# A fused attention, mixture-of-experts and feed-forward kernel: weight pieces kept in DRAM, work moved from GpSimd to VectorE, and plain products in half of the output layers

## The chip, the cores and the metric

The kernel runs on one core of a Trainium2 chip. A core has TensorE (PE, matmuls, with PEld its weight loads), VectorE (DVE), ScalarE (ACT), GpSimd (POOL) and SyncE (SP, which issues transfers); each works through its own queue in order. The metric is the device time of one execution in microseconds, and less is better.

## The reference

Three layers follow each other. Linear attention gives x of 2304 tokens by 512; four experts, weighted by probabilities, give the next x; a feed-forward layer with a sigmoid gate gives the output.

```python
q_s = softmax(q over the head dim);  k_s = softmax(k over the sequence)
x   = q_s @ (k_s.T @ v)                          # 4 batches, 8 heads of 64, 576 tokens
p   = domain_probs / domain_probs.sum(-1)
x   = sum over e of p[:, e] * (relu(x @ w1[e]) @ w2[e])    # 4 experts, 512 -> 1024 -> 512
h   = x @ w_in                                   # 512 -> 2048
out = (h * sigmoid(1.702 * h)) @ w_out           # 2048 -> 512
```

w_in and w_out arrive as 64-bit floats.

## The kernel before, in words

Tokens are taken in three passes of 768 (`TP`), each as two halves of 384 (`N`). Weights are taken in units of 512 hidden columns: eight units a pass in the expert layers (`moe`, two for an expert), four in the last layer (`ffn`), so 24 + 12 = 36 units. A unit is a first layer (`mm1`, two halves of 256 hidden columns) and an output layer (`mm2`, two halves `dt` of 256 output columns).

Each half multiplies a 2x2 arrangement of weight blocks (a11 to a22) by a 2x2 arrangement of activations (b11 to b22). It does so with seven block products where eight would be the plain way: sums of weights s1 to s4 (`MADE`) and of activations t1 to t4 (`TSUM`) take part, `ORDER` (L111) lists the products with the PSUM bank that each adds to ("x", "z" or "y"), and a bank is read several times while products add up in it. For accuracy every factor is split into a rounded part and its residue: ScalarE casts (`hi`), and a subtraction gives the rest (`lo`). A product is six matmuls of 128x128 by 128x384 (`product`, L117): two blocks of the inner dimension times high-high, high-low and low-high.

`weights_of` (L136) makes the pieces of a half. At the first pass GpSimd makes the sums s1 to s4, ScalarE casts all seven pieces, DVE makes the residues of the sums and of a22, GpSimd those of a11 and a12, and the four sums' pieces are stored to DRAM. At the later passes the raw block is loaded again, the four sums are reloaded ready-made, and a11, a12 and a22 are cast and their residues made by GpSimd again. `x_forms` (L209) and `h_forms` (L300) do the like for activations: seven casts, seven residues on DVE, and t1 and t2 on DVE and t3 and t4 on GpSimd for the hidden ones.

The outputs of `mm2` add up in `acc` over the units of an expert (first copies on ScalarE, adds on DVE); `weigh` multiplies by the probabilities on GpSimd and `total` adds to `tot` on DVE.

In the background of the expert passes run the attention for the later tokens and the decoding of w_in and w_out to 32 bits (32 tiles, seven DVE operations and a GpSimd add each). Generators give them out a turn at a time; `pump` asks for the next turn. All attention turns, the transposes of the output and the "y" products share three "y" banks.

The order is written by hand: `at(place, fn)` puts work on a plan in steps, a step being one product of each layer, and the plan is sorted by place and emitted as it is. `mm2` runs 4 steps (`LAG`) behind the unit's end, so the output layer of one unit and the first layer of the next alternate on PE. A piece's steps are given relative to the step that uses it:

```python
at(slot - 11, load)
...
            if x in MADE:
                if again:
                    at(s - 6, reload, x)
                    continue
                at(s - 7, make, x, SUM_ENG[x])
            at(s - 5, hi, x)
            at(s - 3.9, lo, x, (LO_AGAIN if again else LO_ENG)[x])
            if x in MADE:
                at(s - 2.2, store, x)
```

Of the kernel before, what the change touches and what calls it, by code (L numbers as in the profile page):

```python
# [22 lines left out]
def tile_linear_attention_moe_gelu(  # L23
# [49 lines left out]
    BANKS = {"x": 3, "z": 2, "y": 3}  # L73
# [43 lines left out]
    def product(st, i, weights, forms, nm):  # L117
        w, f, b, first = ORDER[i]
        if first:
            st[b] = bank(b, [P, N], f"{b}{nm}")  # L120
        (wh, wl), (xh, xl) = weights.pop(w), forms[f]
        n = 0
        for kk in range(2):
            for l, r in ((wh, xh), (wh, xl), (wl, xh)):
                T.matmul(  # L125
                    st[b], l[:, kk, :], r[:, kk, :], start=(first and n == 0), stop=(n == 5),
                    skip_group_check=True,
                )
                n += 1
# [6 lines left out]
    def weights_of(key, nm, src, slot):  # L136


        got, y, made = {}, {}, {}
        again = key in kept  # L140
        names = [x[0] for x in ORDER]

        def load():
            y["raw"] = rawp.tile([P, KT, 256], F32, tag="raw", name=f"raw{nm}")
            S_.dma_start(out=y["raw"], in_=src.rearrange("(c p) f -> p c f", p=P))

        def block(x):
# [24 lines left out]
        def store(x):  # L172
            d = dram.tile([P, 512], F32, name=f"k_{x}_{nm}")
            kept[key][x] = d
            S_.dma_start(out=d, in_=y[x])

        def reload(x):
            flat = new(x)
            S_.dma_start(out=flat, in_=kept[key][x])

        at(slot - 11, load)
        for i, x in enumerate(names):
            s = slot + i
            if x in MADE:
                if again:
                    at(s - 6, reload, x)
                    continue
                at(s - 7, make, x, SUM_ENG[x])
            at(s - 5, hi, x)
            at(s - 3.9, lo, x, (LO_AGAIN if again else LO_ENG)[x])  # L190
            if x in MADE:
                at(s - 2.2, store, x)
        if not again:
            kept[key] = {}
        return got

    SUM_ENG = {"s1": G, "s2": G, "s3": G, "s4": G}
    LO_ENG = {"a11": G, "s1": V, "s2": V, "a12": G, "s3": V, "s4": V, "a22": V}
    LO_AGAIN = {"a11": G, "a12": G, "a22": G}
# [9 lines left out]
    def x_forms(pas_key, nm, slot, source, S=G):  # L209
# [26 lines left out]
        at(slot - 2.6, make, "t3", G, "b12")  # L236
# [16 lines left out]
    def mm1(kx, layer, pas, half, slot, weights):  # L253
# [29 lines left out]
        for i in range(7):  # L283
            at(slot + i, lambda i: product(st, i, weights, X[layer, pas], nm), i)
# [15 lines left out]
    def h_forms(kx, s1):  # L300

        forms = Hf[kx] = {}
        place = {}

        def src(f):
            return U[kx, place.get(f, f)]

        def hi(f):
            forms[f] = form_tiles(pools["hp", "p"], f, f"_{kx}")
            A.copy(forms[f][0], src(f))  # L310

        def lo(f, eng):
            tt(eng, forms[f][1], src(f), forms[f][0].bitcast(F32), ALU.subtract)
# [6 lines left out]
        at(s1 + 6.20, hi, "b11")  # L320
        at(s1 + 6.70, lo, "b11", V)
        at(s1 + 7.30, make, "t1", V, "b11")
        at(s1 + 7.35, make, "t3", G, "b12")
        at(s1 + 7.90, hi, "t1")
        at(s1 + 8.30, lo, "t1", V)
        at(s1 + 9.30, make, "t2", V, "b11")
        at(s1 + 9.80, hi, "t2")
        at(s1 + 10.30, lo, "t2", V)
        a, b = ("t3", "b21") if kx + 1 < len(seq) else ("b21", "t3")
        at(s1 + 10.80, hi, a)  # L330
        at(s1 + 11.30, lo, a, V)
        at(s1 + 11.80, hi, b)
        at(s1 + 12.30, lo, b, V)
        at(s1 + 12.80, hi, "b22")
        at(s1 + 12.85, make, "t4", G, "b21")
        at(s1 + 13.30, lo, "b22", V)
        at(s1 + 14.00, hi, "t4")
        at(s1 + 14.40, lo, "t4", V)
# [10 lines left out]
    def mm2(kx, layer, pas, u, dt, slot, weights):  # L349
# [18 lines left out]
        for i in range(7):  # L368
            at(slot + i + 0.5, lambda i: product(st, i, weights, Hf[kx], nm), i)
        for i, (r, t, b) in enumerate(  # L370
            ((0, 0, "x"), (1, 1, "z"), (0, 1, "x"), (0, 0, "y"), (1, 1, "x"), (0, 1, "z"), (1, 0, "x"))
        ):
            at(slot + i + 1.05, add, r, t, b)
# [11 lines left out]
        def total(r):  # L385
            kk = 2 * dt + r
            if e:
                o = acc[dt, r].rearrange("p t n -> p (t n)")
                tt(V, tot[pas][:, kk, :], tot[pas][:, kk, :], o, ALU.add)
            if e == E - 1:  # L390
                S_.dma_start(out=x_d["ffn", pas][:, kk, :], in_=tot[pas][:, kk, :])

        def turn(x, eng):

            y = bank("y", [SP, 2, 2, P], f"o{nm}_{x}")
# [7 lines left out]
            S_.dma_start(  # L403
# [6 lines left out]
        if layer == "moe" and last:  # L410
            for r, s in ((0, 6.3), (1, 7.4)):
                at(slot + s, weigh, r)
                at(slot + s + 3 + 0.9 * r, total, r)
        if layer == "ffn" and last:
            for n, x in enumerate((2, 3, 0, 1)):
                at(slot + (6.6, 7.2, 7.6, 7.9)[n], turn, x, V if n % 2 and kx == len(seq) - 1 else A)
# [3 lines left out]
    seq = [(layer, p, u) for layer, n in (("moe", E * FE // FU), ("ffn", FF // FU)) for p in range(NPASS) for u in range(n)]  # L420
    begins = {}
    for kx, (layer, pas, u) in enumerate(seq):
# [3 lines left out]
        if layer == "moe":  # L426
            e, f0 = divmod(u * FU, FE)
            wa, wb = w1[e], w2[e]
        else:
            f0, wa, wb = u * FU, wi32, wo32  # L430
        for half in range(2):
            sl = s0 + 7 * half
            got = weights_of(
                (layer, u, 1, half), f"a{kx}_{half}", wa[:, f0 + half * 256 : f0 + (half + 1) * 256],
                sl if kx else START + 17 + 7 * half,
            )
            mm1(kx, layer, pas, half, sl, got)
        h_forms(kx, s0 + 7)
        for dt in range(2):
# [3 lines left out]
            got = weights_of((layer, u, 2, dt), f"b{kx}_{dt}", wb[f0 : f0 + FU, dt * 256 : (dt + 1) * 256], sl)  # L443
            mm2(kx, layer, pas, u, dt, sl, got)
        if layer == "moe" and u % 2 == 0:
            at(s0 + 18, load_p, u // 2, pas)


    def attend(b, j, c0, nc_, keys):
# [14 lines left out]
        def bk(n, s):  # L464
            return bank(ATTN_BANK[early].get(n, "y"), s, f"{n}_{nm}")

# [170 lines left out]
        def group(g):  # L637
# [16 lines left out]
            def xf(eng):  # L654
# [39 lines left out]
    ATTN_BANK = {True: {"kT0": "x", "kT1": "x", "kb0": "z", "kb1": "z"}, False: {}}  # L694
# [28 lines left out]
    def probabilities():  # L723
# [13 lines left out]
        def turn(x):  # L737
            w = 4 * SP
            y = bank("y", [E, w], f"pt{x}")
# [4 lines left out]
            S_.dma_start(out=pt_d[:, x * w : (x + 1) * w], in_=o)  # L744
# [52 lines left out]
    def attention(todo):  # L797
# [12 lines left out]
        while live:  # L810
# [4 lines left out]
            if todo and len(live) < 2 and (not live or len(live[0]) == 4):  # L815
                nxt = load(todo.pop(0))
                live.append([(nxt[0][0], "")] * 2 + nxt)
# [48 lines left out]
    def decode_all(part):  # L866
# [4 lines left out]
        for n, x in enumerate(todo):  # L871
            if n + 1 < len(todo):
                next(todo[n + 1])
            for stage, _ in enumerate(x):
                yield
                if stage == 1 and late:
# [75 lines left out]
```

## Time and profile before

| | |
|---|---|
| median of 3 runs | 1468.76 us (1466.09 to 1469.67) |
| the profiled execution | 1470.22 us, its span 1468.4 us |
| mean granted TensorE clock | 0.931 |
| instructions | 21252 |
| DMA | 292.46 MB, mean 199 GB/s |

The span is the time from the first to the last instruction. Busy time is the time in which an engine executes; waiting, branching and issuing transfers don't count. In a window of the trace the busy time of each engine can be set beside the window's length. An operation's duration can overlap the next one's start on the same engine, so the sum of durations is more than the busy time.

### The profile page before, as it was taken

The numbers are of one execution on the slowest core, as the hardware profiler recorded it, in microseconds if no ns is written. First come the engines' busy times: TensorE is split into PE (matmuls) and PEld (weight loads), VectorE is DVE, ScalarE is ACT, GpSimd is POOL, SyncE is SP. The second block draws the span as 40 slices with busy tenths as digits, with TensorE's granted clock in tenths as the row PEclk, the third lists the DMA queues.
The fourth block names the chain that finished last, engine by engine and source line by source line (L and its number), as shares of the span: only waits on it lengthen the run. The fifth ranks groups of instructions, "written<-read, shape, count | busy, mean of one in ns | idle before, by whom it ended". The sixth has DMA issues, their size and how long they took to land.

```text
span 1468.4 us, 21252 instructions
## 1 busy us (share of the span) xinstructions
PE 1243.8 (85%) x6688; PEld 1191.0 (81%) x6688; DVE 1320.2 (90%) x1779; ACT 762.5 (52%) x1715; POOL 963.3 (66%) x805
## 2 busy tenths in 40 slices
PE   7778878797798997778877778998888779989998
PEld 6677877697798987778867777997788679989997
DVE  6779999999998889999999999878999997898787
ACT  5566564474655653344534344555565546555653
POOL 5267877778856765658665665769876754564552
PEclk8799988899899998899988989999989999999999
DMA  8145555455568786668667766775455547776773
GB/s 222 57 160 179 195 173 168 141 190 182 188 205 261 222 283 206 191 229 269 192 205 266 244 212 212 224 240 170 157 181 172 201 143 252 216 234 202 224 214 86
DMA packets 208383, 292.46 MB, mean 199 GB/s; under 512 B 34296, under 2 KB 122640, under 8 KB 207632
## 3 DMA queue, kind: packets, MB, share of 16 engines
q1 hardware_dynamic: 208272, 291.11, 62.1%
q8 instruction: 53, 0.87, 0.2%
q14 instruction: 58, 0.48, 0.1%
HBM read 219.71 MB, written 71.34 MB: 198 GB/s over the span
## 4 chain that ended last, share of the span: by engine, by line
DVE 49%; PE 32%; issue 9%; ACT 4%; POOL 3%; DMA 2%; SPq 0%; DVEq 0%; POOLq 0%; ACTq 0%
PE x L125 18%; PE z L125 8%; DVE acc L108 6%; DVE b L108 6%; PE y L125 4%; DVE t1l L108 3%; DVE s_a L108 3%; DVE s_b L108 2%; DVE t3l L108 2%; DVE tot L108 2%; DVE b11l L108 2%; DVE t2l L108 2%; DVE b22l L108 1%; DVE e L108 1%; DVE p L108 1%
## 5 line engine op out<-in xcount | busy, mean ns | idle before, releaser
L108 POOL TENSOR_TENSOR b<-b,b 128x768 f32<-128x768 f32 x72 | 139.2, 1933 | 201.3 <-DVE b21l L108 113.8
L108 POOL TENSOR_TENSOR a_b<-rawb,a_b 128x256 fp32r<-128x256 f32 x192 | 209.6, 1092 | 42.3 <-ACT a_b L166 42.2
L108 POOL TENSOR_TENSOR a_a<-rawa,a_a 128x256 fp32r<-128x256 f32 x192 | 204.0, 1062 | 17.8 <-ACT a_a L166 16.4
L125 PE MATMUL x<-t4h,a_b 128*128 128x384 f32 x288 | 97.5, 380 | 70.5 <-DVE acc L108 70.2
L125 PE MATMUL x<-t3h,s_b 128*128 128x384 f32 x288 | 92.6, 363 | 39.5 <-DVE acc L108 32.2
L125 PEld LDWEIGHTS x<-t4h,a_b 128*128 128x128 f32 x288 | 58.9, 208 | 81.6 <-DVE acc L108 81.5
L108 DVE TENSOR_TENSOR acc<-x,acc 128x384 f32<-128x384 f32 x198 | 108.1, 546 | 10.6 <-PE x L125 10.2
L125 PE MATMUL x<-t4h_moe,a_a 128*128 128x384 f32 x192 | 63.5, 372 | 49.0 <-DVE e L108 49.0
L125 PE MATMUL x<-t2h,s_b 128*128 128x384 f32 x288 | 94.5, 370 | 5.7 <-DVE acc L108 4.4
L125 PEld LDWEIGHTS x<-t3h,s_b 128*128 128x128 f32 x288 | 55.8, 197 | 48.9 <-DVE acc L108 35.6
L310 ACT CAST t2h<-b 128x768 fp32r<-128x768 f32 x36 | 30.1, 837 | 119.8 <-DVE b L108 119.8
L125 PE MATMUL x<-b11h,a_b 128*128 128x384 f32 x288 | 91.3, 358 | 0.0
L108 POOL TENSOR_TENSOR acc<-acc,pb 128x768 f32<-128x768 f32 x36 | 73.6, 2049 | 26.6 <-DVE acc L108 26.6
L166 ACT CAST a_a<-rawa 128x256 fp32r<-128x256 f32 x216 | 86.9, 402 | 0.0
L166 ACT CAST a_b<-rawb 128x256 fp32r<-128x256 f32 x216 | 86.9, 403 | 0.0
L125 PE MATMUL z<-b22h,s_b 128*128 128x384 f32 x288 | 86.5, 341 | 0.0
L125 PE MATMUL z<-t1h,s_b 128*128 128x384 f32 x288 | 84.9, 335 | 0.1
L125 PE MATMUL y<-b21h,a_b 128*128 128x384 f32 x288 | 84.8, 335 | 0.0
L125 PEld LDWEIGHTS x<-t4h_moe,a_a 128*128 128x128 f32 x192 | 37.8, 200 | 55.7 <-DVE e L108 55.5
L276 ACT ACTIVATE b<-p 128x384 f32<-128x384 f32 x48 | 25.2, 526 | 106.3 <-DVE p L108 106.2
L108 DVE TENSOR_TENSOR b<-b,b 128x768 f32<-128x768 f32 x72 | 79.1, 1098 | 0.1
L108 DVE TENSOR_TENSOR acc<-z,acc 128x384 f32<-128x384 f32 x114 | 62.3, 547 | 18.0 <-PE z L125 17.9
(266 smaller groups left out, 4700.7 us busy)
## 6 DMA issues: line engine op xcount, KB each, us to landing
s_a<-k_s_a SPq DMA_DIRECT2D x192, 256.0 KB, 3.9
s_b<-k_s_b SPq DMA_DIRECT2D x192, 256.0 KB, 3.8
rawa<-in_moe_w SPq DMA_DIRECT2D x48, 512.0 KB, 5.3
k_s_a<-s_a SPq DMA_DIRECT2D x96, 256.0 KB, 2.3
rawb<-in_moe_w SPq DMA_DIRECT2D x48, 512.0 KB, 5.7
k_s_b<-s_b SPq DMA_DIRECT2D x96, 256.0 KB, 2.5
rawa<-wi SPq DMA_DIRECT2D x24, 512.0 KB, 4.9
rawb<-wo SPq DMA_DIRECT2D x24, 512.0 KB, 4.3
```

The source lines that it names most:

```text
L108: eng.tensor_tensor(out=o, in0=a, in1=b, op=op)
L125: T.matmul(st[b], l[:, kk, :], r[:, kk, :], start=(first and n == 0), stop=(n == 5), skip_group_check=True,)
L166: A.copy(got[x][0], block(x))
L276: A.activation(dest(u), c, AF.Relu)
L310: A.copy(forms[f][0], src(f))
```

## The change

It has six parts.

1. Weight pieces. Every piece that a later pass needs is stored to DRAM when it is first made, a11 to a22 too, and later passes reload all of them (`again`, `have`). The raw block is loaded only where a piece is missing. Sums and residues of weights are all made on DVE.
2. Output layer. Only 18 of the 36 units (`SEVEN`) keep the seven products in `mm2`; the others take eight plain products in the order `PLAIN`, two to a bank, which need only the four blocks of either factor and four reads of banks, not seven. Passes 2 and 3 of the experts have seven products from their third unit on, the last two passes of the last layer from their second.
3. Engines. The hidden sums t3 and t4 go from GpSimd to DVE, `total` from DVE to GpSimd. ScalarE issues the stores of attention results, of probabilities and of most of the output.
4. PSUM. "y" has two banks for three, and one bank "w" serves the background attention, the probabilities and the transposes of the output.
5. Background. Ten of the 32 decode tiles are decoded in the first expert pass, the rest in the third (before: 14 in the second, 18 in the third); the numbers of turns in each unit are listed (`PUMPS`); a head's turns start a turn later.
6. Buffers: 16 weight pieces for 15, 5 sums for 6, 6 bank copies for 7.

The diff, cut:

```diff
-    wp = ctx.enter_context(tc.tile_pool(name="wp", bufs=15))
+    wp = ctx.enter_context(tc.tile_pool(name="wp", bufs=16))
-    sump = ctx.enter_context(tc.tile_pool(name="sump", bufs=6))
-    evp = ctx.enter_context(tc.tile_pool(name="evp", bufs=7))
+    sump = ctx.enter_context(tc.tile_pool(name="sump", bufs=5))
+    evp = ctx.enter_context(tc.tile_pool(name="evp", bufs=6))
-    BANKS = {"x": 3, "z": 2, "y": 3}
+    BANKS = {"x": 3, "z": 2, "y": 2, "w": 1}
...
+    QUARTERS = ((0, 0), (1, 0), (0, 1), (1, 1))
+    PLAIN = tuple(
+        (f"a{r + 1}{c + 1}", f"b{c + 1}{t + 1}", ("x", "z", "y", "y'")[i], c == 0)
+        for i, (r, t) in enumerate(QUARTERS) for c in range(2)
+    )
...
-    def weights_of(key, nm, src, slot):
+    def weights_of(key, nm, src, slot, order, pitch, again):
...
-        again = key in kept
-        names = [x[0] for x in ORDER]
+        have = kept.setdefault(key, {})
+        need = {}
+        for i, step in enumerate(order):
+            need.setdefault(step[0], slot + pitch * i)
...
-        def make(x, eng):
+        def make(x):
...
-            tt(eng, o, block(l), block(r), op)
+            tt(V, o, block(l), block(r), op)
...
-        def lo(x, eng):
+        def lo(x):
             h, l = got[x]
-            tt(eng, l, block(x), h.bitcast(F32), ALU.subtract)
+            tt(V, l, block(x), h.bitcast(F32), ALU.subtract)
...
-        at(slot - 11, load)
-        for i, x in enumerate(names):
-            s = slot + i
+        if any(x not in have for x in need):
+            at(slot - 11, load)
+        for x, s in need.items():
+            if x in have:
+                at(s - 5, reload, x)
+                continue
             if x in MADE:
-                if again:
-                    at(s - 6, reload, x)
-                    continue
-                at(s - 7, make, x, SUM_ENG[x])
-            at(s - 5, hi, x)
-            at(s - 3.9, lo, x, (LO_AGAIN if again else LO_ENG)[x])
-            if x in MADE:
-                at(s - 2.2, store, x)
+                at(s - 6.2, make, x)
+            at(s - 4.4, hi, x)
+            at(s - 3.2, lo, x)
+            if x in again:
+                at(s - 1.0, store, x)
...
-    def h_forms(kx, s1):
+    def h_forms(kx, s1, seven, after_seven):
...
+        if not seven:
+            for s, f in ((7.2, "b11"), (8.4, "b21"), (10.8, "b12"), (11.9, "b22")):
+                at(s1 + s, hi, f)
+                at(s1 + s + 0.5, lo, f)
+            return
...
-        at(s1 + 7.35, make, "t3", G, "b12")
+        at(s1 + d + 7.80, make, "t3", V, "b12")
...
-        at(s1 + 12.85, make, "t4", G, "b21")
+        at(s1 + 12.95, make, "t4", V, "b21")
...
+        else:
+            for i, step in enumerate(PLAIN):
+                at(slot + 0.875 * i + 0.5, product, st, step, weights, Hf[kx], nm, not step[3])
+            for i, (r, t) in enumerate(QUARTERS):
+                at(slot + 1.75 * i + 2.3, lambda r, t, i: add(r, t, PLAIN[2 * i][2]), r, t, i)
...
-                tt(V, tot[pas][:, kk, :], tot[pas][:, kk, :], o, ALU.add)
+                tt(G, tot[pas][:, kk, :], tot[pas][:, kk, :], o, ALU.add)
...
-            y = bank("y", [SP, 2, 2, P], f"o{nm}_{x}")
+            y = bank("w", [SP, 2, 2, P], f"o{nm}_{x}")
...
-            S_.dma_start(
+            (A if eng is A else S_).dma_start(
...
+    SEVEN = {("moe", 1): range(2, 8), ("moe", 2): range(2, 8), ("ffn", 1): (1, 2, 3), ("ffn", 2): (1, 2, 3)}
...
+        again = [x[0] for x in ORDER] if pas + 1 < NPASS else []
...
+        later = {
+            x[0] for p in range(pas + 1, NPASS) for x in (ORDER if u in SEVEN.get((layer, p), ()) else PLAIN)
+        }
...
-            return bank(ATTN_BANK[early].get(n, "y"), s, f"{n}_{nm}")
+            return bank(ATTN_BANK[early].get(n, "y" if early else "w"), s, f"{n}_{nm}")
...
-                    S_.dma_start(out=x_d["moe", pas][:, j, i : i + m], in_=o[:, d - t0 : d - t0 + m])
+                    A.dma_start(out=x_d["moe", pas][:, j, i : i + m], in_=o[:, d - t0 : d - t0 + m])
...
-    CUT = 14
-    at(moe1 + 3, lambda: bg.append(decode_all(tiles[:CUT])))
+    CUT = 10
+    at(moe0 + 3, lambda: bg.append(decode_all(tiles[:CUT])))
     at(moe2 + 3, lambda: bg.append(decode_all(tiles[CUT:])))
-    for s in range(moe0 + 3, ffn0 - 11):
-        at(s + 0.93, pump)
-        if s >= moe1 and s % 14 in (7, 9, 11):
-            at(s + 0.45, pump)
+    PUMPS = [18, 18, 18, 18, 15, 15, 15, 15] + [22, 22, 14] + [14] * 5 + [18, 18] + [16] * 6
+    for kx, n in enumerate(PUMPS):
+        for i in range(n):
+            s = 14 * kx + (i + 0.5) * 14 / n
+            if not -11 <= s - begins[seq[kx][:2]] < 3 and not (seq[kx][:2] != seq[kx + 1][:2] and s > 14 * kx + 3):
+                at(s, pump)
```

## Rows read from the trace of the kernel before

**Rows 1.** The page, part 1: busy us (share of the span) and instructions.
```profile
PE 1243.8 (85%) x6688; PEld 1191.0 (81%) x6688; DVE 1320.2 (90%) x1779; ACT 762.5 (52%) x1715; POOL 963.3 (66%) x805
```

**Rows 2.** Windows, one per unit: bounds, length, busy time of each engine.
```profile
core 0: us, PE busy (x) PEld busy (x) DVE busy (x) ACT busy (x) POOL busy (x), PEclk, DMA share, GB/s
217.90:263.10 45.20, 38.03 (x197) 35.92 (x196) 44.56 (x57) 22.70 (x55) 32.45 (x30) 0.89 0.52 166
...
948.20:977.30 29.10, 29.10 (x170) 29.10 (x169) 20.26 (x29) 16.64 (x36) 19.32 (x16) 1.00 0.74 216
...
1310.20:1348.10 37.90, 32.05 (x185) 30.63 (x185) 32.11 (x43) 20.79 (x43) 19.09 (x16) 1.00 0.56 162
1348.10:1379.30 31.20, 31.20 (x187) 30.86 (x186) 23.19 (x32) 20.31 (x45) 15.60 (x15) 1.00 0.78 239
...
1408.40:1468.40 60.00, 53.14 (x309) 50.96 (x307) 47.29 (x70) 23.74 (x46) 23.91 (x19) 1.00 0.46 134
```

**Rows 3.** Windows, one per pass: opening, three expert passes, three of the last layer.
```profile
0.00:58.30 58.30, 43.42 (x289) 38.41 (x289) 37.25 (x106) 31.91 (x93) 26.68 (x35) 0.85 0.65 176
58.30:388.60 330.30, 269.46 (x1393) 253.95 (x1394) 311.18 (x400) 185.59 (x446) 246.07 (x222) 0.89 0.52 168
388.60:704.00 315.40, 270.11 (x1445) 260.62 (x1444) 293.09 (x379) 154.97 (x336) 210.73 (x164) 0.94 0.71 228
704.00:1011.80 307.80, 258.00 (x1347) 247.74 (x1346) 280.70 (x346) 142.05 (x305) 203.91 (x153) 0.93 0.68 222
1011.80:1174.50 162.70, 131.82 (x673) 125.94 (x672) 156.97 (x214) 88.89 (x205) 124.12 (x107) 0.93 0.52 177
1174.50:1310.20 135.70, 125.47 (x707) 122.77 (x706) 113.92 (x161) 77.46 (x164) 76.75 (x64) 0.97 0.69 219
1310.20:1468.40 158.20, 145.49 (x845) 141.55 (x844) 127.08 (x179) 81.67 (x168) 75.01 (x63) 1.00 0.59 177
```

**Rows 4.** The list of waits: who waited for whom, us in total, times, longest.
```profile
PE x L125 <- DVE acc L108: 106.8, 57, 6.0
...
PE x L125 <- ACT acc L364: 7.6, 6, 2.1
```

**Rows 5.** Timeline of DVE, from 1097.8 us: start, us, engine, line, operation.
```profile
1097.99 0.42 DVE L108 TENSOR_TENSOR s_a<-s3s_a,s_a 128x256 fp32r<-128x256 f32 x1
1098.33 0.95 DVE L108 TENSOR_TENSOR b<-b,b 128x768 f32<-128x768 f32 x1
1099.19 0.55 DVE L108 TENSOR_TENSOR acc<-y,acc 128x384 f32<-128x384 f32 x1
1099.66 1.82 DVE L108 TENSOR_TENSOR s_b<-s1s_b,s_b 128x256 fp32r<-128x256 f32 x1
```

**Rows 6.** Timeline of GpSimd over the same stretch.
```profile
1099.36 1.85 POOL L108 TENSOR_TENSOR b<-b,b 128x768 f32<-128x768 f32 x1 [3.27 <-DVE b L108]
```

**Rows 7.** Decode lines L845 and L841, two of seven: duration ns min/median/max.
```profile
L845 DVE TENSOR_SCALAR dti<-w64i x16: 410/418/1824, 528.5 to 736.0; 128x512 int32<-128x512 int32 x16
...
L841 DVE SCALAR_TENSOR_TENSOR dsi<-w64i,dsi x16: 691/693/2221, 527.5 to 734.0; 128x512 int32<-128x512 int32 x16
```

**Rows 8.** Groups by shape on GpSimd: count, busy us, mean ns, idle before.
```profile
L108 POOL TENSOR_TENSOR a_b<-rawb,a_b 128x256 fp32r<-128x256 f32 x192 | 209.6, 1092 | 42.3 <-ACT a_b L166 42.2
...
L108 POOL TENSOR_TENSOR b<-b,b 128x768 f32<-128x768 f32 x72 | 139.2, 1933 | 201.3 <-DVE b21l L108 113.8 <-DVE b L108 79.9 <-PE x L125 5.4
...
L108 POOL TENSOR_TENSOR acc<-acc,pb 128x768 f32<-128x768 f32 x36 | 73.6, 2049 | 26.6 <-DVE acc L108 26.6
```

**Rows 9.** DMA queues, and issues by line with median us to landing.
```profile
q1 hardware_dynamic: 208272, 291.11, 62.1%
...
s_a<-k_s_a SPq DMA_DIRECT2D x192, 256.0 KB, 3.9
```

More of the change, by code (lines that the diff above doesn't have):

```diff
@@ L115, in tile_linear_attention_moe_gelu, with product @@
     )
-    def product(st, i, weights, forms, nm):
-        w, f, b, first = ORDER[i]
+    QUARTERS = ((0, 0), (1, 0), (0, 1), (1, 1))
[3 more added lines that the diff above has]
+    )
+    def product(st, step, weights, forms, nm, last=True):
+        w, f, b, first = step
         if first:
-            st[b] = bank(b, [P, N], f"{b}{nm}")
-        (wh, wl), (xh, xl) = weights.pop(w), forms[f]
+            st[b] = bank(b[0], [P, N], f"{b[0]}{nm}")
+        (wh, wl), (xh, xl) = weights[w], forms[f]
         n = 0
@@ L125, in product @@
                 T.matmul(
-                    st[b], l[:, kk, :], r[:, kk, :], start=(first and n == 0), stop=(n == 5),
+                    st[b], l[:, kk, :], r[:, kk, :], start=(first and n == 0), stop=(last and n == 5),
                     skip_group_check=True,
@@ L235, in x_forms @@
         at(slot - 3.6, make, "t2", S, "b11")
[L236 removed]
+        at(slot - 2.6, make, "t3", S, "b12")
         at(slot - 2.5, hi, "t2")
@@ L283, in mm1 @@
         for i in range(7):
-            at(slot + i, lambda i: product(st, i, weights, X[layer, pas], nm), i)
+            at(slot + i, lambda i: product(st, ORDER[i], weights, X[layer, pas], nm), i)
         at(slot + 0.55, read, "p1", "x")
@@ L347, in load_p, with mm2 @@
         )
-    def mm2(kx, layer, pas, u, dt, slot, weights):
+    def mm2(kx, layer, pas, u, dt, slot, weights, seven):
         st = {}
@@ L366, in add @@
                 tt(V, o, st[b], o, ALU.add)
[L368 to L373, printed above, removed]
+        if seven:
+            for i in range(7):
+                at(slot + i + 0.5, lambda i: product(st, ORDER[i], weights, Hf[kx], nm), i)
+            for i, (r, t, b) in enumerate(
+                ((0, 0, "x"), (1, 1, "z"), (0, 1, "x"), (0, 0, "y"), (1, 1, "x"), (0, 1, "z"), (1, 0, "x"))
+            ):
+                at(slot + i + 1.05, add, r, t, b)
+        else:
[3 more added lines that the diff above has]
+                at(slot + 1.75 * i + 2.3, lambda r, t, i: add(r, t, PLAIN[2 * i][2]), r, t, i)
         def weigh(r):
@@ L410, in mm2 @@
         if layer == "moe" and last:
-            for r, s in ((0, 6.3), (1, 7.4)):
-                at(slot + s, weigh, r)
-                at(slot + s + 3 + 0.9 * r, total, r)
+            for r in range(2):
+                at(slot + 6.4 + 1.3 * r, weigh, r)
+                at(slot + 6.5 + 1.3 * r, total, r)
+                if e == E - 1:
+                    at(slot + 9.2 + 1.8 * r, keep, r)
         if layer == "ffn" and last:
-            for n, x in enumerate((2, 3, 0, 1)):
-                at(slot + (6.6, 7.2, 7.6, 7.9)[n], turn, x, V if n % 2 and kx == len(seq) - 1 else A)
+            for n, x in enumerate((2, 3, 0, 1) if seven else (0, 1, 2, 3)):
+                s = (6.6, 7.2, 7.6, 7.9)[n] if kx == len(seq) - 1 else 6.6 + 0.7 * n
+                at(slot + s, turn, x, V if n % 2 and kx == len(seq) - 1 else A)
     START = -44.0
     seq = [(layer, p, u) for layer, n in (("moe", E * FE // FU), ("ffn", FF // FU)) for p in range(NPASS) for u in range(n)]
+    SEVEN = {("moe", 1): range(2, 8), ("moe", 2): range(2, 8), ("ffn", 1): (1, 2, 3), ("ffn", 2): (1, 2, 3)}
     begins = {}
+    after_seven = False
     for kx, (layer, pas, u) in enumerate(seq):
@@ L430, in tile_linear_attention_moe_gelu @@
             f0, wa, wb = u * FU, wi32, wo32
+        seven = u in SEVEN.get((layer, pas), ())
+        again = [x[0] for x in ORDER] if pas + 1 < NPASS else []
         for half in range(2):
@@ L442, in tile_linear_attention_moe_gelu @@
                 sl = s0 + 14 + (1.5, 4)[dt]
-            got = weights_of((layer, u, 2, dt), f"b{kx}_{dt}", wb[f0 : f0 + FU, dt * 256 : (dt + 1) * 256], sl)
-            mm2(kx, layer, pas, u, dt, sl, got)
+            got = weights_of(
+                (layer, u, 2, dt), f"b{kx}_{dt}", wb[f0 : f0 + FU, dt * 256 : (dt + 1) * 256], sl,
+                ORDER if seven else PLAIN, 1 if seven else 0.875, later,
+            )
+            mm2(kx, layer, pas, u, dt, sl, got, seven)
         if layer == "moe" and u % 2 == 0:
-            at(s0 + 18, load_p, u // 2, pas)
+            at(s0 + 22, load_p, u // 2, pas)
     def attend(b, j, c0, nc_, keys):
@@ L738, in turn @@
             w = 4 * SP
-            y = bank("y", [E, w], f"pt{x}")
+            y = bank("w", [E, w], f"pt{x}")
             for c in range(4):
@@ L814, in attention @@
             yield
-            if todo and len(live) < 2 and (not live or len(live[0]) == 4):
+            if todo and len(live) < 2 and (not live or len(live[0]) == 3):
                 nxt = load(todo.pop(0))
-                live.append([(nxt[0][0], "")] * 2 + nxt)
+                live.append([(nxt[0][0], "")] + nxt)
         close_pool("attn")
@@ L871, in decode_all @@
         for n, x in enumerate(todo):
-            if n + 1 < len(todo):
-                next(todo[n + 1])
             for stage, _ in enumerate(x):
                 yield
-                if stage == 1 and late:
+                if stage == 0 and n + 1 < len(todo):
+                    next(todo[n + 1])
+                if stage == 2 and late:
                     late.pop(0)()
```

68 lines of the change are left out of this document (35 added, 33 removed).

## Prediction

> **What bounds the kernel now.** I read the page's engine totals first [rows 1]: VectorE (DVE) is busy 1320 us of 1468, TensorE (PE) 1244. Then I cut the span into its 36 weight units (512 hidden columns each) and set busy time beside length [rows 2]. Two kinds of unit show. Where DVE is nearly full, the unit is as long as DVE's work: 45.2 us with DVE 44.6. Where DVE has room, PE sets the length: 29.1 us with DVE at 20.3, every matmul back to back. That unit has 28 products of 6 matmuls, so a matmul costs 29.1 / 168 = 0.173 us, and a unit with 16 transposes besides takes 31.2, so 2.1 / 16 = 0.13 us for a small PE operation. The granted clock falls below 1 only where PE waits. By pass [rows 3] DVE is 91 to 96% busy in the three expert passes and in the first pass of the last layer; the last two passes are nearly PE's. The list of waits agrees: PE waits longest for DVE's adds [rows 4].
>
> Why is DVE full? Two neighbouring pieces of its timeline tell [rows 5, 6]. A 128x256 subtraction of SBUF operands took 0.42 us, and the next instruction started 0.34 us after it. Another one took 1.82 us: it began at 1099.66, inside a GpSimd operation of 1.85 us that began at 1099.36, and ended 0.27 us after that. The 128x768 sum between them took 0.95 us, with the next start 0.86 later. The adds that read PSUM beside it took 0.55, 0.47 from start to start, as everywhere. So DVE's SBUF work has a quiet price and pays on top when GpSimd is in the way. I use the distance between starts as the price, since neighbours overlap by some 0.08 us: 0.33 (128x256), 0.87 (128x768), 0.47 (128x384 from PSUM). The seven decode operations have minima of 0.41 to 0.69 [rows 7], 3.2 us a tile after the same deduction.
>
> **DVE after.** Weight pieces: there are 48 blocks. Before, DVE made 5 residues for each at first use, 240 operations. After, the 24 first-layer blocks cost 4 sums and 7 residues once (264); the 18 output blocks that use both schemes 4 residues for plain products and later 4 sums and 4 residues (216); the 6 plain ones 4 (24). 504 x 0.33 = 167 us. Hidden forms: 18 units x 11 + 18 x 4 = 270 against 324 before, x 0.87 = 234. Output adds: a plain half has 4, not 7, so 384 - 36 x 3 = 276, x 0.47 = 129. First-layer adds 216 x 0.47 = 101; gates 96 x 0.47 = 45; 42 x-form residues and 3 sums x 0.87 = 39; decode 32 x 3.2 = 103; attention and the rest unchanged, about 88 (DVE's busy time less the groups named). The 36 `total` additions leave. Quiet sum 906 us. The same sum for the kernel before is 946, so the other 374 of its 1320 us are what GpSimd costs DVE.
>
> **What GpSimd still takes.** Of its costliest groups [rows 8] the 384 weight residues, the 192 weight sums and the 72 hidden sums go. It keeps 48 `weigh` and gets 36 `total` (2.0 us each), 32 decode adds, 21 x-form sums and the attention operations: about 307 us of the 963. Bounds of what that costs DVE: nothing, if DVE always comes first, and 307, if each blocks it throughout. Scaled by GpSimd's time, 307 x 374/963 = 119; I take that, because both kernels mix queued and idle moments. DVE then has 1025 us (906 to 1213). The Trainium skill (SBUF — State Buffer, Who interferes with whom) says that a DVE instruction with two SBUF inputs and a GpSimd instruction that reads SBUF exclude each other for a whole instruction, whoever starts first. The 1.82 us above agrees. What it would make of the sum if GpSimd always came first is the second rival.
>
> **PE after.** A plain half has 8 products for 7: 12 more matmuls in each of 18 units, 2.1 us each, 37 us in all. Nothing covers it where PE is the bound.
>
> **The rest.** ScalarE casts fall from 624 to 336 for weights and 252 to 198 for hidden forms; it issues some 55 DMAs more, which at 52% busy [rows 1] I cost at nothing. Decoding moves: 10 tiles into the first pass, none in the second, 22 in the third; each is counted where it lands. Pieces now come from DRAM on SP's queue: 564 reloads for 384, 318 stores for 192, 66 raw loads for 144, so 39 MB more on 292 and a DMA share of 62 -> 70% [rows 9]. A reload lands in 3.9 us; it is issued five steps of two products, 10.4 us, ahead (six before). A store waiting on SP for its residue holds the reloads behind it, and PE waits for those; with two thirds of the lead left I cost it at nothing, up to 30 us if the cover goes. Fewer spare `sump`, `evp` and "y" buffers: nothing, up to the third rival's price. In the opening 58.3 us [rows 3] the sums of the first unit pass to a DVE with time to spare: unchanged.
>
> **The sum by pass**, each unit the longer of PE and DVE plus about a microsecond; boundary units 4 to 6 more, as the first unit of the last pass shows (37.9 with either engine at 32) [rows 2].
> Expert pass 1: DVE's own work is 18 us a unit (30 pieces 10, forms 3.5, adds 4.7). Attention adds 1.5 heads a unit, 8 us, and GpSimd some 4: 30, under PE's 31.2 + 3. First unit 25, second 30, three of 35.5. Decoding adds 12 (3.75 tiles), and GpSimd's adds, `weigh` and `total` there are 13.8 us a unit, of which 0.39 falls on DVE, 5.4: two units of 36.5, and the boundary 35.5: 270 (330 before).
> Pass 2: three plain units with dense attention 37, 36, 32.5; four with seven products, where DVE has 24 and PE sets 29.8 each; the last 33: 258 (315).
> Pass 3: decoding 22 tiles, not 18. Two plain units 36, 33; then DVE has 9.5 (forms) + 2.8 and 4.7 (adds) + 12.8 (four tiles) + 5.4 for GpSimd, 35.2, so three of 36.5 and one of 35, then 30 and 33: 277 (308).
> Last layer: 135 (PE 31.2 and boundaries; 163 before), 129 (136), 156 (158).
> With the opening: 58 + 270 + 258 + 277 + 135 + 129 + 156 = 1283, and 1.8 us lie outside the span, as before (1470.2 against 1468.4): **1285 us**. The profiled execution stands 0.1% over the median of the runs, so the same figure serves for both.
>
> **Rivals.** *PE everywhere.* If the exclusion costs almost nothing, every unit is PE's: 58 + 6048 x 0.173 + 37 + 350 small operations x 0.13 + 8 at the end (its stretch of 60.0 less 276 matmuls and 32 transposes) + five boundaries of 6.7 = 1228, up to 1262. For it: units with DVE at 30 or less are already at PE's pace. Against: 22 decode tiles in one pass.
> *GpSimd always first.* Each of its operations then stops DVE for its whole length. The six units that decode get 13.8 instead of 5.4 us each, 50 more: 1335. For it: the 1.82 us in rows 5. Against: the quiet 0.42 and 0.95 us there, and GpSimd's queue, which after the change is mostly empty. The Trainium skill's rule above allows both orders.
> *The lone bank.* Background attention and the output transposes get one PSUM bank, "w", for three shared "y", and plain halves take two turns on two "y" banks that the first layer also uses. PE is in order, so it stands until the bank is read. Where PE waited for ScalarE to read a bank it lost 7.6/6 = 1.27 us [rows 4]. 102 uses of "w" and 36 plain halves could cost 175 us; half gives 1373 (1345 to 1425). Against: the turns of the background are spaced so that few follow directly. The Trainium skill (Perfetto Trace Analysis, Matmuls) wants independent groups to rotate through banks for this reason; no row shows one bank in this use.
> *The price stays (slower).* If the slow DVE operations come from something other than GpSimd, each of the 1115 SBUF operations after keeps the mean surcharge of 374/940 = 0.40 us: 446 + 906 = 1352, 32 us over now, so 1502. It decides from 0.37 us a piece, where DVE is back at 1320. Against it stand rows 5 and 6.
>
> **Numbers.** Forecast 0.62 (1262 to 1325), PE everywhere 0.12, GpSimd first 0.07, lone bank 0.14, price stays 0.05. The range runs from 1238, inside the first rival, to 1372, inside the third; outside lie about 0.03 below and 0.12 above, and I go no narrower because ScalarE's and SP's part is costed at nothing. A difference under 0.3% can't be told from none; faster 0.95, same 0.01, slower 0.04.
>
> **What would show it.** Right: DVE near 1000 to 1050 us busy, GpSimd near 300, 128x256 subtractions mostly at 0.41, units of the second pass at 30 us with the granted clock at 1, decode units of the third still DVE's. Wrong: PE waiting for the reader of a "w" or "y" bank, or for a reload; 128x256 operations still near 0.9 us; ScalarE over 80% in the first pass.

## Result and profile after

The changed kernel takes 1350.6 us (median of 4 runs, 1348.8 to 1353.5) against 1469.2 for the kernel before: ratio 0.9196, 95% interval 0.9171 to 0.9221. That is 118.6 us less, inside the whole range (1238 to 1372), 65.6 us more than the forecast of 1285 and above the forecast's own band (1262 to 1325).

The page's engine totals of the changed kernel:

```profile
PE 1230.6 (91%) x6904; PEld 1190.8 (88%) x6904; DVE 1092.1 (81%) x1846; ACT 645.1 (48%) x1373; POOL 316.7 (23%) x192
```

Beside [rows 1]: DVE fell by 228 us (forecast 1025, it is 67 over that), GpSimd by 647 to 317 (forecast 307). The windows by pass, columns as in [rows 2]; the first is the opening:

```profile
0.00:57.90 57.90, 44.22 (x289) 39.70 (x289) 40.13 (x118) 32.21 (x93) 18.38 (x23) 0.82 0.76 217
57.90:366.80 308.90, 273.21 (x1471) 260.30 (x1472) 259.04 (x462) 160.47 (x385) 90.17 (x55) 0.93 0.70 232
366.80:632.40 265.60, 258.27 (x1487) 253.47 (x1486) 199.81 (x317) 133.94 (x270) 75.52 (x45) 0.99 0.78 257
632.40:918.10 285.70, 253.73 (x1370) 246.55 (x1370) 264.19 (x373) 111.56 (x211) 98.60 (x54) 0.95 0.81 277
918.10:1055.30 137.20, 125.47 (x703) 122.76 (x703) 119.04 (x224) 76.01 (x174) 24.57 (x13) 0.99 0.76 256
1055.30:1186.10 130.80, 127.52 (x737) 124.83 (x736) 93.76 (x165) 63.64 (x124) 7.52 (x4) 1.00 0.71 237
1186.10:1349.50 163.40, 148.20 (x857) 143.24 (x855) 116.12 (x193) 67.24 (x121) 1.91 (x1) 0.99 0.64 207
```

Forecast by pass: 58, 270, 258, 277, 135, 129, 156. The opening and the last layer's first two passes came within some 2 us. Pass 1 is 39 us over, pass 2 is 8, pass 3 is 9 and the last pass 7. Against [rows 3] the gains are 21, 50 and 22 us in the expert passes, 26 and 5 in the next two, and a loss of 5 in the last.

Four units of the changed kernel, cut as in [rows 2]: one with decoding in pass 1, the last of that pass, one with seven products in pass 2, and the first of the last layer.

```profile
237.90:280.10 42.20, 34.72 (x182) 33.10 (x182) 41.82 (x73) 17.50 (x44) 14.34 (x8) 0.92 0.66 222
...
318.90:366.80 47.90, 37.27 (x182) 35.67 (x181) 39.58 (x62) 21.10 (x49) 19.76 (x12) 0.88 0.68 239
...
568.80:597.90 29.10, 29.10 (x170) 29.10 (x169) 25.50 (x44) 15.41 (x31) 7.34 (x4) 1.00 0.83 284
...
918.10:956.80 38.70, 30.61 (x169) 28.86 (x169) 38.15 (x62) 20.69 (x43) 9.64 (x5) 1.00 0.75 251
```

The first and the last are still DVE's: DVE is busy for all but 0.4 to 0.6 us of them. The third is PE's at the forecast 29.1. The second is neither's: DVE has 8 us of slack and PE 11. The list of waits of the whole run (who waited for whom, us in total, times, longest; the first line is GpSimd idle until its next work is ready):

```profile
POOL acc L108 <- DVE acc L108: 209.3, 18, 37.7
...
PE x L131 <- DVE acc L108: 28.3, 17, 3.1
...
PE x L131 <- DVE e L108: 26.3, 15, 5.0
...
PE y L131 <- DVE acc L108: 14.8, 5, 5.7
...
PE kT L607 <- DMA k<-in_k: 1.9, 1, 1.9
```

PE's wait for DVE's adds out of bank "x" fell from 106.8 us [rows 4] to 28.3. A wait for "y" banks, which the forecast costed at nothing and named as a sign of being wrong, has come in: 13 waits on DVE's and ScalarE's `acc`, 20 us. Matmuls wait for a transfer once, 1.9 us, in the attention; no weight reload holds them, at a DMA share of 72.2% (forecast 70).

What GpSimd still costs DVE is best seen at the end of an expert, where its two `weigh` and two `total` stand in a row. The DVE timeline of the changed kernel, and GpSimd's over the same stretch (start, us, engine, line, operation):

```profile
338.87 2.61 DVE L108 TENSOR_TENSOR t3l<-b,t3h 128x768 fp32r<-128x768 f32 x1
341.40 0.55 DVE L108 TENSOR_TENSOR acc<-y,acc 128x384 f32<-128x384 f32 x1
341.86 0.54 DVE L108 TENSOR_TENSOR e<-x,e 128x384 f32<-128x384 f32 x1
342.33 1.11 DVE L108 TENSOR_TENSOR s_a<-s1s_a,s_a 128x256 fp32r<-128x256 f32 x1
343.36 2.07 DVE L108 TENSOR_TENSOR s3s_a<-rawa 128x256 f32<-128x256 f32 x1
345.35 2.59 DVE L108 TENSOR_TENSOR b22l<-b,b22h 128x768 fp32r<-128x768 f32 x1
```

```profile
338.62 2.04 POOL L108 TENSOR_TENSOR acc<-acc,pb 128x768 f32<-128x768 f32 x1
340.74 2.42 POOL L108 TENSOR_TENSOR tot<-tot,acc 128x768 f32<-128x768 f32 x1
343.11 2.03 POOL L108 TENSOR_TENSOR acc<-acc,pb 128x768 f32<-128x768 f32 x1
345.22 1.91 POOL L108 TENSOR_TENSOR tot<-tot,acc 128x768 f32<-128x768 f32 x1
```

The two engines take turns by whole operations. Each DVE operation on SBUF alone that starts inside a GpSimd one ends 0.3 to 0.8 us after it; the two that read PSUM (0.55, 0.54) keep their usual length. DVE needs 9.1 us (338.87 to 347.94) for what costs 0.87 x 2 + 0.33 x 2 + 0.47 x 2 = 3.3 in quiet: 5.7 us for 8.4 of GpSimd's, a share of 0.68 where the forecast used 0.39.

### The profile page after: what moved, and what is told of

It is laid out like the page before. It is cut to its first block, busy times and chain, and to the rows that moved or that the text cites. A ratio compares the mean times of both kernels' runs of the same rounds, so it can differ in the third digit from the quotient of the medians.

```text
span 1349.5 us, 20618 instructions
## 1 busy us (share of the span) xinstructions
PE 1230.6 (91%) x6904; PEld 1190.8 (88%) x6904; DVE 1092.1 (81%) x1846; ACT 645.1 (48%) x1373; POOL 316.7 (23%) x192
## 3 DMA queue, kind: packets, MB, share of 16 engines
q1 hardware_dynamic: 202912, 323.33, 72.2%
## 4 chain that ended last, share of the span: by engine, by line
PE 53%; DVE 34%; issue 4%; DMA 4%; ACT 3%; POOL 1%; SPq 0%; ACTq 0%; DVEq 0%; POOLq 0%
PE x L131 24%; PE z L131 13%; PE y L131 12%; DVE b L108 4%; DVE acc L108 4%; DVE s_b L108 2%; DVE s_a L108 1%; PE pk L653 1%; DVE b21l L108 1%; DVE a_a L108 1%; DVE b11l L108 1%; DVE t3l L108 1%; DVE a_b L108 1%; PE px L687 1%; DVE e L108 1%
## 5 line engine op out<-in xcount | busy, mean ns | idle before, releaser
L131 PE MATMUL y<-b22h,a_b 128*128 128x384 f32 x288 | 88.9, 349 | 0.0
L131 PE MATMUL y<-t3h,a_b 128*128 128x384 f32 x288 | 86.4, 340 | 0.0
L108 DVE TENSOR_TENSOR p<-y,p 128x384 f32<-128x384 f32 x72 | 39.6, 550 | 52.6 <-PE y L131 52.5
L131 PE MATMUL y<-b21h_moe,a_a 128*128 128x384 f32 x192 | 61.5, 362 | 18.8 <-DVE acc L108 13.8
L108 POOL TENSOR_TENSOR tot<-tot,acc 128x768 f32<-128x768 f32 x36 | 72.7, 2019 | 2.8
L131 PE MATMUL x<-t3h,s_b 128*128 128x384 f32 x144 | 45.0, 353 | 19.8 <-DVE acc L108 13.3
L131 PE MATMUL x<-t2h_moe,s_a 128*128 128x384 f32 x192 | 59.9, 353 | 2.3 <-ACT p L266 2.3
L131 PE MATMUL x<-b11h_moe,a_a 128*128 128x384 f32 x192 | 60.7, 357 | 1.3 <-ACT b11h_moe L226 1.3
L131 PE MATMUL x<-t3h_moe,s_a 128*128 128x384 f32 x192 | 58.7, 347 | 1.9 <-ACT u L266 1.9
L131 PE MATMUL z<-t1h_moe,s_a 128*128 128x384 f32 x192 | 57.8, 342 | 1.3 <-DVE u L108 1.3
```

The source lines that it names most:

```text
L108: eng.tensor_tensor(out=o, in0=a, in1=b, op=op)
L131: T.matmul(st[b], l[:, kk, :], r[:, kk, :], start=(first and n == 0), stop=(last and n == 5), skip_group_check=True,)
```

## Experiments

All times are medians of 4 runs beside the kernel before on the same chip (1469 to 1470 us); the ratio to it stands with its interval. The theory that they test is that the mechanism of the forecast holds (each unit is the longer of PE and DVE) and the 65 us are sizes, the price of what GpSimd keeps above all; the rivals are the lone bank, the place of the decoding, and that work which was moved, or pieces which were kept, brought nothing. The letters are explained in each expectation.

**The banks.** Three "y" banks again, shared by all.

```diff
-    BANKS = {"x": 3, "z": 2, "y": 2, "w": 1}
+    BANKS = {"x": 3, "z": 2, "y": 3}
```

(and "y" for "w" where it is named)

> The changed kernel with the old banks: three shared "y", no "w". Theory A (what is over the forecast is DVE's work and its waits for GpSimd): PE's waits for a reader of a "y" or "w" bank are DVE's lateness seen at another bank and move elsewhere; 1345 to 1355 us, ratio 0.916 to 0.923. Theory B (the lone bank and the two "y" banks): the 22 us of waits for "y" and some 8 us for "w" go, 1320 to 1330 us, ratio 0.898 to 0.906.

Measured: 1332.7 us, ratio 0.9073 [0.9059, 0.9086]: 18 us faster than the changed kernel, 3 us above B's range. Half of it is in pass 1 (299.2 for 308.9), and half of that in the last unit, 42.9 for 47.9. That unit, and one line of the waits:

```profile
313.90:356.80 42.90, 34.10 (x182) 33.46 (x181) 39.10 (x61) 20.01 (x46) 18.10 (x10) 0.90 0.69 243
```

```profile
PE x L131 <- DVE e L108: 46.9, 18, 8.0
```

So the bank split costs 18 us, not the 88 that the prediction gave the rival. The list of waits doesn't show these 18: the 20 us for "y" banks go, but the waits for DVE's `e` rise from 26.3 to 46.9, as A said, and PE's idle time falls by only 3 us (118.9 to 115.7). DVE's busy time is the same, 1092.0. The other 15 us are PE's busy time, 1230.6 to 1215.8 with the same 6904 matmuls. About half of that is the clock: in the changed kernel 83 us of PE's busy time lie at the lower granted level, 0.50, and here 69, which makes 7 us. The 47.9 us unit shows how: PE stood from 327.0 to 332.3 us for a "y" bank, the granted clock was 0.50 from 331 to 337, and PE then did 8 matmuls in 2 us, against 13 or 14 at 1.00. Later it stood for a "y" bank again, 3.3 us, and the clock fell again; with three banks this unit has one stop, of 8.0 us, and 5.0 us of busy time at 0.50 in place of 10.2. What makes up the other half isn't shown.

**`weigh` and `total` on DVE.** Both leave GpSimd, 84 operations of 128x768.

```diff
-                tt(G, tot[pas][:, kk, :], o, pb[e, pas], ALU.mult)
+                tt(V, tot[pas][:, kk, :], o, pb[e, pas], ALU.mult)
...
-                tt(G, o, o, pb[e, pas], ALU.mult)
+                tt(V, o, o, pb[e, pas], ALU.mult)
...
-                tt(G, tot[pas][:, kk, :], tot[pas][:, kk, :], o, ALU.add)
+                tt(V, tot[pas][:, kk, :], tot[pas][:, kk, :], o, ALU.add)
```

> The changed kernel with weigh and total on DVE, so 84 GpSimd operations fewer. DVE gets 84 x 0.87 = 73 us of quiet work. Theory A1 (GpSimd mostly goes first and each of these operations costs DVE 1.0 to 2.3 us, 149 us as the trace after adds up): DVE busy falls from 1092 to about 1020, time 1310 to 1335 us, ratio 0.892 to 0.909. Theory A2 (the forecast's 0.39 us per GpSimd us, 66 us): DVE busy stays near 1095, time 1348 to 1360.

Measured: 1320.9 us, 0.8995 [0.8977, 0.9014], 30 us faster. The page:

```profile
PE 1218.5 (92%) x6904; PEld 1180.7 (90%) x6904; DVE 1072.2 (81%) x1930; ACT 644.8 (49%) x1373; POOL 149.4 (11%) x108
```

DVE does 84 operations more, 73 us at 0.87, and is busy 20 us less. On GpSimd they had cost it 93 us, 1.1 each; the forecast's 0.39 of 2.0 us gave 0.78, or 65 in all, and A1's 149 was too much.

**Only `total` on DVE**, as before the change: the last of these three edits alone.

> Only the adds of `total` (36 operations of 128x768) go back from GpSimd to VectorE; the weighing stays on GpSimd. Putting both back was worth 30 us. Theory A (the price of what GpSimd keeps is the third of the misses, and `total` carries most of it, since VectorE pays 2.26 us for each of its 36 operations there, 81 us, against 0.87 us, 31 us, to do the adds itself): about 1330 us (1325 to 1338), VectorE's sum 30 to 50 us lower than the 1092. Theory B (the weighing, which stands ahead of `total` in GpSimd's queue and which the next unit's accumulators wait for, carries it): 1344 to 1352, no change to speak of.

Measured: 1350.4 us, 0.9171 [0.9145, 0.9198]: nothing. Its page, and one wait:

```profile
PE 1231.3 (91%) x6904; PEld 1191.9 (88%) x6904; DVE 1059.4 (78%) x1882; ACT 645.6 (48%) x1373; POOL 241.6 (18%) x156
```

```profile
DVE tot L108 <- POOL acc L108: 38.6, 22, 3.0
```

DVE's busy time falls by 33 us, as A said, and the time doesn't: DVE now stands 38.6 us in its queue waiting for `weigh`, which stayed on GpSimd and has to end first. A was right on the price and wrong on the time; B had the time, and this wait, as long as what DVE was spared, is the likely reason. Taken in this order, the 36 totals had cost DVE 64 us (33, and 31 for doing the adds itself), 1.8 each, and the 48 weighs the other 29 of the 93, 0.6 each. `weigh` alone on DVE wasn't tried.

**Weight sums and residues on GpSimd again** (168 sums, and the 96 residues of a11 and a12).

```diff
-            tt(V, o, block(l), block(r), op)
+            tt(G, o, block(l), block(r), op)
...
-            tt(V, l, block(x), h.bitcast(F32), ALU.subtract)
+            tt(G if x in ("a11", "a12") else V, l, block(x), h.bitcast(F32), ALU.subtract)
```

> The changed kernel with the 168 weight sums and the 96 residues of a11 and a12 on GpSimd again, 264 operations of 128x256, about 1 us each. DVE is relieved of 264 x 0.33 = 87 us of quiet work. Theory A (the two engines exclude each other): DVE's surcharge rises by 90 to 130 us, DVE busy stays at 1090 to 1130, and the chain of sum, cast and residue gets longer: 1350 to 1385 us. Theory F (the slow DVE operations had another cause): DVE busy falls to about 1005 us, time 1290 to 1320.

Measured: 1349.6 us, 0.9184 [0.9170, 0.9198]: no change.

```profile
PE 1225.7 (91%) x6904; PEld 1185.2 (88%) x6904; DVE 1065.3 (79%) x1582; ACT 644.9 (48%) x1373; POOL 549.1 (41%) x456
```

264 operations leave DVE, 87 us in quiet, and its busy time falls by 27: they cost it 60 us from GpSimd, 0.23 each. A had the time but put DVE 25 to 65 us too high; F is refuted. For the time it made no difference where these operations run. The Trainium skill (SBUF — State Buffer, Who interferes with whom) says that the loser of the shared ports stands for the whole instruction of the other; the timelines above show that, and this run shows that it need not be the price of every instruction: 0.23 us for a 128x256 operation on GpSimd, 1.1 for a 128x768 one in a row of four.

**Only the sums kept in DRAM.** The blocks a11 to a22 are made from the raw block in every pass, now on ScalarE and DVE.

```diff
-            if x in again:
+            if x in again and x in MADE:
...
-            if x in need and x not in have:
+            if x in need and x not in have and x in MADE:
```

> Only the four sums are kept in DRAM, as in the kernel before; a11, a12 and a22 are loaded raw again in the later passes, cast on ScalarE and their residues made again, now on VectorE: some 300 operations of 128x256 more on VectorE at 0.33 us, 99 us, and as many casts on ScalarE at 0.4 us, 120 us. Theory A (in passes 2 and 3 VectorE has 270 to 290 us in 285 to 300, so that the units that it bounds grow by its work and those that TensorE bounds hide it): 1385 us (1370 to 1400). Theory B (the stores and reloads in DRAM cost about what they save, as the transfers are 40 MB more): 1345 to 1355. Theory C (all of the 99 us is on the path): 1440 to 1450.

Measured: 1412.4 us, 0.9610 [0.9593, 0.9627]: 62 us slower than the changed kernel.

```profile
PE 1249.1 (89%) x6904; PEld 1200.9 (85%) x6904; DVE 1208.8 (86%) x2146; ACT 733.9 (52%) x1673; POOL 316.6 (22%) x192
```

300 operations more on DVE cost it 117 us, 0.39 each. About half of that is time. In pass 2, where most units are PE's, 40 us more of DVE's work cost 14 us (279.8 for 265.6); in pass 3, with DVE the bound, another 40 cost 32 (317.6 for 285.7). The 300 casts more on ScalarE, 89 us, aren't separated from this. The time lies between A's and C's figures and refutes B.

**Seven products everywhere**, all 36 units.

```diff
-    SEVEN = {("moe", 1): range(2, 8), ("moe", 2): range(2, 8), ("ffn", 1): (1, 2, 3), ("ffn", 2): (1, 2, 3)}
+    SEVEN = {(l, p): range(8) for l in ("moe", "ffn") for p in range(3)}
```

> The changed kernel with the seven products in the output layer of all 36 units. PE gets 37 us less; DVE 126 x 0.87 + 108 x 0.47 + 24 x 0.33 = 168 us more. Theory A (each unit is the longer of PE and DVE): the units of the first expert pass get 9 us more each, the first pass of the last layer 20 in all; 1430 to 1460 us, no faster than 3% before the change. Theory E (PE sets the end): about 1315 us.

Measured: 1429.6 us, 0.9732 [0.9713, 0.9751], at the lower edge of A's range: 79 us slower.

```profile
PE 1222.8 (86%) x6688; PEld 1173.3 (82%) x6688; DVE 1258.6 (88%) x2104; ACT 681.9 (48%) x1427; POOL 334.1 (23%) x192
```

DVE has 166 us more; 18 units x (7 x 0.87 + 6 x 0.47) gives 160. So plain products in half of the units are the largest part of the gain, though PE does 216 matmuls more.

**Plain products everywhere** (`SEVEN = {}`).

> The changed kernel with eight plain products in the output layer of all 36 units. PE gets 18 x 2.1 = 37 us more, DVE 126 x 0.87 + 108 x 0.47 + 144 x 0.33 = 208 us less. Theory A (each unit is the longer of PE and DVE): units of the second pass 31.2 instead of 29 to 33, decoding units of the third 33 to 34 instead of 36 to 41; 1330 to 1348 us. Theory D (DVE sets the end nearly everywhere): about 1260 us. Theory E (PE sets the end nearly everywhere): 1350 + 37 = 1387 us.

Measured: 1317.4 us, 0.8966 [0.8952, 0.8981]: 33 us faster than the changed kernel, where A had expected 3 to 21 (1330 to 1348). Of this 25 us are in pass 3 (260.7 for 285.7), where DVE has 61 us less to do, and 8 in the last layer's first pass (129.1 for 137.2). Pass 2 (265.0 for 265.6) and the last two passes stay as they were, with more matmuls.

**The first ten decode tiles in pass 2**, not in pass 1.

```diff
-    at(moe0 + 3, lambda: bg.append(decode_all(tiles[:CUT])))
+    at(moe1 + 3, lambda: bg.append(decode_all(tiles[:CUT])))
```

> The changed kernel with the first ten decode tiles in the second expert pass and not in the first. Theory A (DVE is over in the decoding units): the first pass falls from 309 to about 280 us, the second rises from 266 by 15 to 25, together 1335 to 1350 us. Theory C (the first pass is long for its weight chains, banks and ScalarE, not for the decoding): the first pass stays above 298 us and the total rises to 1355 to 1375.

Measured: 1355.3 us, 0.9233 [0.9217, 0.9248]. Pass 1 falls by 28 us to 280.5, as A said, and pass 2 rises by 29 to 294.8, more than A's 15 to 25: two of its units with seven products now take 43 us, with DVE busy for all but 0.4 of them (29.2 and 33.0 before). C had the time, but it had pass 1 stay above 298 us, and that is refuted.

**The parts put together.** Banks and `weigh` with `total` on DVE:

> The changed kernel with three shared "y" banks and with weigh and total on DVE. If the two shares are apart, 18 and 30 us add up: 1302 us (1296 to 1308). If PE's waits for a bank are the same lateness of DVE that GpSimd's operations cause: 1312 to 1321.

Measured: 1305.5 us, 0.8888 [0.8868, 0.8908]: 18 and 30 add up (45). Its first three windows after the opening:

```profile
57.10:348.00 290.90, 261.10 (x1471) 253.33 (x1472) 247.34 (x482) 160.73 (x385) 51.30 (x35) 0.95 0.73 243
348.00:607.00 259.00, 255.07 (x1487) 252.18 (x1486) 201.70 (x344) 132.76 (x269) 19.16 (x16) 1.00 0.81 269
607.00:883.60 276.60, 248.63 (x1370) 241.74 (x1369) 257.47 (x401) 112.08 (x212) 41.11 (x26) 0.98 0.83 285
```

Passes 2 and 3 now stand where the forecast had them (258, 277), and pass 1 alone is 21 over. Its first two units and its last:

```profile
57.10:87.10 30.00, 23.02 (x117) 20.08 (x118) 21.42 (x34) 16.88 (x37) 6.64 (x5) 0.83 0.24 79
87.10:122.40 35.30, 31.69 (x177) 30.43 (x178) 25.17 (x54) 23.86 (x63) 8.56 (x6) 0.95 0.78 257
...
304.50:348.00 43.50, 33.28 (x182) 32.96 (x181) 38.48 (x66) 21.10 (x49) 11.29 (x7) 0.88 0.66 235
```

The same with plain products everywhere:

> As the one before, and eight plain products in every unit. Every unit should be PE's: 58 + 6048 x 0.173 + 75 for the added products + 46 for small operations + 8 at the end + boundaries of 25 to 35 us = 1258 to 1268. If the three shares overlap, 1285 to 1300.

Measured: 1280.7 us, 0.8715 [0.8699, 0.8732], between the two ranges: not every unit became PE's, as pass 1 still takes 291.8 us. Then with the decode tiles in pass 2 as well, and last with seven products again in the eight units that have nothing in the background (`SEVEN = {("moe", 1): (6, 7), ("ffn", 1): (1, 2, 3), ("ffn", 2): (1, 2, 3)}`):

> The best version so far (three banks for y and none apart, weighing and totals on VectorE, plain products in every output layer; 1280.7 us) with the ten decode tiles in the second expert pass in place of the first. There the first pass is 291.8 us for eight units of 31.2 us (250 us), the second 263.1. Theory A (in the second pass VectorE has room under TensorE, as the weights' pieces are reloaded): first pass 268 to 275, second 265 to 275, the whole 1262 to 1270. Theory B (a decode tile costs what it costs in whatever pass, as it did in the changed kernel, where the move took 28 us out of the one pass and put 29 us into the other): 1277 to 1285.

> The version with the decode tiles in the second pass, with seven products in the output layer of the units that have nothing in the background: the last two units of the second expert pass and three units in each of the last two passes of the last layer, 8 units, 8 x 12 = 96 matmuls, 16.6 us of TensorE at 0.173 us. Theory A (those units are TensorE's, at 31.2 us plain and 29.1 us with seven): 12 to 17 us below the version with plain products everywhere. Theory B (the seven reads of banks and the sums bring back waits that eat this): within 5 us of it.

Measured: 1258.4 us, 0.8561 [0.8543, 0.8579], and 1268.1, 0.8622 [0.8608, 0.8635]. The first is the best of all, 92 us below the changed kernel; its theory A held (pass 1 268.8, pass 2 263.0), and the time is 4 us better than its range. Its totals, and the same last unit of pass 1 as above:

```profile
PE 1224.9 (97%) x7120; PEld 1207.8 (96%) x7120; DVE 863.9 (69%) x1552; ACT 590.6 (47%) x1247; POOL 138.8 (11%) x108
```

```profile
296.30:327.50 31.20, 31.20 (x182) 31.20 (x181) 25.11 (x43) 20.12 (x46) 7.01 (x4) 1.00 0.91 307
...
590.50:621.70 31.20, 31.20 (x182) 31.20 (x181) 24.37 (x38) 12.07 (x22) 3.33 (x3) 1.00 0.66 208
```

The same 182 matmuls that took 37.27 us now take 31.20. For the version with eight units of seven products both theories missed; it is 10 us slower. The second row above is the first unit of pass 3; with seven products in the unit before, it is

```profile
589.20:630.80 41.60, 32.64 (x171) 31.03 (x170) 41.23 (x70) 17.56 (x36) 4.58 (x3) 0.94 0.54 173
```

where DVE, busy for all but 0.4 us, has the forms of the new pass, `weigh` and `total` and the seven reads of the old unit together. The six such units of the last layer bring 1.1 us together (129.2 and 159.4 us for the two passes, against 128.8 and 160.9); the two where the second expert pass ends cost 11, 2 in that pass and 9 in the next.

## Why the prediction came out so

**What bounds the kernel: right in the main.** Undisturbed units with room on DVE run at 29.1 or 31.2 us as predicted, and decoding units as long as DVE is busy. Neither holds for the 47.9 us unit. PE's extra 37 us are there: 31.2 for 29.1 in the plain units. The time alone would have misled: 1350.6 lies in the band of the rival *lone bank* (1345 to 1425), and only the runs show that the banks are 18 us of it. That the whole range holds it is in part luck: its upper end, 1372, came from that rival's price, and the miss has three parts, of which the banks are one.

**Where the gain comes from**, by undoing one part at a time in the changed kernel:

| part undone | us slower than the changed kernel |
|---|---|
| plain products in 18 units | 79 |
| the blocks a11 to a22 kept in DRAM beside the sums | 62 |
| ten decode tiles in pass 1, not 2 | 5 (the two intervals overlap) |
| weight sums and residues on DVE | -1 |
| `total` on GpSimd | 0 |
| banks 2 and 1 for 3 | -18 |

The sum is 127, for 119 measured; parts undone one at a time need not add up, and the move of t3 and t4, 36 operations, the buffers and the new issuers of the stores weren't tried alone. So, as far as tried, the change gains by work that is no longer done, not by work moved from GpSimd to DVE. The prediction's argument, that DVE falls as GpSimd gets out of its way, holds for DVE's busy time: by its quiet sums the surcharge fell from 374 to 186 us. But the moves by themselves brought no time: with the weights' operations on GpSimd again DVE is busy 27 us less, with `total` on DVE again 33 us less, and the kernel takes as long.

**The step that was mis-sized first:** "Scaled by GpSimd's time, 307 x 374/963 = 119". The prediction took GpSimd's queue as mostly empty after the change; but the change puts four operations of 2 us in a row at the end of each expert. For these 84 the share is 0.55, 93 us for 65, and taking them away gave 30 us. Of DVE's 67 us over the forecast these are 28; the other 39 aren't located, and part may be the quiet sum, which was never measured as a whole. The rival *GpSimd always first* priced this kind of blocking, in the decoding units, at 50.

**The step costed at nothing:** "Fewer spare sump, evp and "y" buffers: nothing". The banks cost 18 us. The rival *lone bank* had the place right, and its price wrong: it took half of 138 uses as waits, and 13 waits for "y" banks are listed. Nor is the cost PE's standing time, as the rival had it: that fell by 3 us when the banks came back.

**The rest** of the 65 us, 20, is in pass 1, as the run with both repaired shows. There its last unit, with decoding and the next pass's forms in it, takes 43.5 us; the forecast gave it 35.5. With plain products everywhere it takes 42.3, and without the decoding besides 31.2 (above). The first two units were forecast at 25 and 30 and took 30.0 and 35.3: in the first PE is busy 23.0 us of 30, and its largest wait, 3.3 us in two, is for GpSimd's `qn` in the attention. What sets the length of these two wasn't tried. A decode tile itself was costed nearly right: moving ten of them in the last versions takes 41.1 us of DVE from pass 1 (248.8 to 207.7), 4.1 us a tile, where the forecast had 3.2 and 0.55 for GpSimd's add.

**Right as costed:** the opening (57.9 for 58), ScalarE (48% busy), SP's queue and DMA. 128x256 subtractions are at 0.42 us in the median, as forecast, but a group such as the first sum's residue at 0.76 in the mean. *PE everywhere* did not come about by itself; in the best version, PE's 97% and 1258 us lie at its upper bound of 1262, though with 216 matmuls more than it counted. *The price stays* fell: the mean surcharge went with GpSimd's work, 0.40 us to 0.17 (186 over 1115 operations).

## What to carry to other kernels

Before moving work between two engines that block each other, compare the quiet price on one with the surcharge from the other: for small operations they were near each other here (0.33 and 0.23 us), and moving them gave no time. Long operations in a row on the blocking engine cost more than their share of busy time, and moving only the second of two dependent steps saved busy time and no time. An algorithm that saves matmuls by extra sums pays only where the engine of the sums has room; here the version without it was the faster in all three pairs of runs (18 units twice, 8 units once).

## What the runs showed of the hardware

In these runs a 128x256 operation on GpSimd cost DVE 0.23 us of its 0.9 (mean of 264), and a 128x768 one in a row 1.1 of 2.0 (mean of 84). The exclusion is by whole operations in both directions: GpSimd's `total`, begun beside DVE's 2.61 us residue, took 2.42 for a median of 1.90, and where DVE was idle GpSimd's 128x768 operations took 1.85. PE can pay for a wait a second time: in the unit of 47.9 us, 182 matmuls took 37.27 us of busy time, and 31.20, all at the upper of the two levels of 2.4 and 1.2 GHz, once nothing stopped it. Of the 37.27, 10.2 lie at the lower level behind the two stops and at the unit's start, which makes 5 of the 6 us. So PE's busy time can fall when waits go, with the same matmuls.
